# An adaLN block with linear attention and a GEGLU feed-forward: where the raw W_down transfers run, how many weight buffers gate/up has, and which queue loads the down weights

## The chip, the cores and the metric

The kernel runs on one core of one Trainium2 chip, as one program in one launch. The metric is the time of an execution in microseconds (us), read from the device. Several runs are made and their median counts.

A core has TensorE (PE, matmuls into PSUM), VectorE (DVE), ScalarE (ACT), GpSimd (POOL) and SyncE (SP, which here only issues DMAs). DMAs that POOL issues run through the "software" queue of the profile, those of SP and ACT through "hardware" queues; sixteen DMA engines serve all of them. Every engine works through its own instructions in order, so an instruction or a DMA issue that waits holds up all that stand behind it on that engine.

## The reference

S = 2048 rows, D = 1024, F = 3584, 32 heads of 32, all inputs bf16:

```python
mod = (_silu(c) @ w_mod).reshape(c.shape[0], 6, 1, -1)
sa, ca, ga, sb, cb, gb = (mod[:, 0].copy(), ..., mod[:, 5].copy())
h = _layernorm(x, axis=-1) * (1 + ca) + sa
x = x + ga * _A_ref(h, A_wqkv, A_wo)          # linear attention, phi = elu + 1
h = _layernorm(x, axis=-1) * (1 + cb) + sb
x = x + gb * _B_ref(h, B_w_gate, B_w_up, B_w_down)

def _B_ref(x, w_gate, w_up, w_down):
    return _gelu(x @ w_gate) * (x @ w_up) @ w_down
```

## The kernel before, in words

**Products.** Most matrix products are computed with seven block products in place of eight (the Strassen-Winograd form). That needs sums and differences of the blocks of both operands, which DVE makes, and sums of the products, which DVE and ACT make while they empty PSUM.

**Stages and their place in time.** The rows are cut into four blocks of 512. In the first stage (to about 160 us) each block's layer norm is followed by its K, V and Q products. `ln1_block(b)`, b = 1 to 3, loads four x tiles (SP, line 543), takes their statistics (DVE, 628 and 630), forms rstd and the bias (POOL, 635, 636 and 767), normalises (ACT, 769), stores the tile to `xa_scr[b]` (a DMA of POOL, 770) and, when all four are stored, loads the block back transposed (a DMA of SP, 771). DVE then scales and shifts it (775), and PE starts the block. Then come the merge of the attention state and the output projection (to about 247), and the feed-forward part for two groups of 1024 rows: `gate_up(0)` (247 to 422), `down_out(0)` (to 503), `gate_up(1)` (to 669), `down_out(1)`.

**Gate/up.** The weights come in 14 blocks of 1 MB, gate and up by turns (`w_unit`, load on SP, line 1295). A block needs four sums, s1 to s4, made on DVE by `tt_op` (550) during the block before. Three places in SBUF, `w_slots`, each hold one block and its four sums, so a block's load waits until PE is done with the block three before. In group 0, DVE also makes the sums of W_down (`wd_sums`): its loads (1066, 1067) stand in SP's queue between the weight loads, and POOL stores the results (1078, 1080). The next group's layer norm (`late_norm`) runs there too: a load on SP (1172), ACT, one POOL step (1179), a store by POOL (1182).

**Raw W_down transfers.** `wd_moves` issues from POOL, without passing SBUF, DMAs that write W_down's quarters into scratch in HBM: for each of two sums, 7 plain copies and 7 accumulating ones of 256 KB, 28 in all (line 1033). Ahead of each batch a one-element POOL copy (1053) reads a marker, so that the batch can't start before the marker's data are there. Fourteen run after block 3's transpose, two more with every second weight block of group 0.

**Down.** `down_out` loads W_down's blocks and their sums into regions that gate/up's buffers held (`quarters`, `W_AT`): `nested` products load seven small blocks on SP (1571), `plain` ones a single block of 1.75 MB (1533). In group 0, the three plain loads of sums ("t1", "t2", "t3") are issued by POOL; all others by SP. Residual tiles come by SP too (1521).

**Order.** The program is recorded as a list and `Plan` orders each engine's instructions: it simulates them forward and back with the costs in `cost`, and sorts by the starts it found. PE's order is that of the program. `plan.ahead` says how long before its due time a load may be placed.

Of the kernel before, what the change touches and what calls it, by code (L numbers as in the profile page):

```python
# [11 lines left out]
BF16 = mybir.dt.bfloat16  # L12
F16 = mybir.dt.float16
# [10 lines left out]
class Plan:  # L24
# [106 lines left out]
    def cost(self, op, outs, ins):  # L131

        size = lambda a: math.prod(d[1] for d in a.ap[1:])
        n = max(size(a) for a in (outs if op.eng == "PE" else outs + ins))
        psum = any(a.tensor.name.startswith("psum") for a in outs + ins)
        wide = any(a.dtype == FP32 and size(a) > 8 for a in outs + ins)
        ptrs = sum(size(a) == 1 for a in ins)
        if op.eng == "PE":
            op.cost = n / 2.4 + 2.5
            op.lat = op.cost + 165  # L140
            if op.fn == "matmul" and outs[0].ap[0][1] <= 32:
                op.cost /= 3.5
        elif op.fn.startswith("dma"):
            a = outs[0]
            op.cost, op.bytes = 1000 if op.eng == "POOL" else 450, math.prod(d[1] for d in a.ap) * (4 if a.dtype == FP32 else 2)
            op.bytes *= 2 if "accum_op" in op.kw else 1
            op.load = a.tensor.name.startswith("mem")
            if op.fn == "dma_start_transpose":
                op.cost, op.bytes = self.transpose
            op.lat = op.cost  # L150
        elif op.eng == "ACT":
            op.cost = (55 if psum else 112) + n / 1.2 + 85 * ptrs
            op.lat = op.cost + 115
            f = op.kw.get("func")
            op.table = "g" if f == AF.Gelu_apprx_tanh else "e" if f in (AF.Exp, AF.Ln) else None
        elif op.eng == "POOL":
            op.cost = 500 if n <= 8 else 250 + n / 0.46
            op.lat = 1800 if n <= 8 else op.cost
        else:
            rate = 1.0  # L160
            if op.fn in ("tensor_scalar", "tensor_scalar_mul", "tensor_scalar_add", "tensor_copy") and not wide:
                rate = 1.0 if psum else 4.0
            elif op.fn == "tensor_tensor" and not wide:
                rate = 2.0
            op.cost = 69 + n / (0.96 * rate) + 61 * ptrs
            op.lat = op.cost + 83

# [118 lines left out]
def kernel(  # L286
# [13 lines left out]
    nc = tc.nc  # L300
    P = 128
# [6 lines left out]
    KD = D // P  # L308
    JF = F // P
    TG = 512  # L310
    NG = S // TG
# [14 lines left out]
    KH = KD // 2  # L326
    NPR = JF // 2
    MW = 4 * NW

    KB = 1024  # L330
    mem_pool = ctx.enter_context(tc.tile_pool(name="mem", bufs=1))
    mem = mem_pool.tile([P, 103 * KB + KB // 2], BF16, name="mem", tag="mem")
    ps_pool = ctx.enter_context(tc.tile_pool(name="psum", bufs=1, space=bass.MemoryType.PSUM))
    psm = ps_pool.tile([P, 8, NW], FP32, name="psum", tag="psum")

# [48 lines left out]
    def at(off, shape, dt):  # L384
        return Ring(off, shape, dt, 1)()
# [61 lines left out]
    hr1 = [h12[b // 2][:, b % 2] for b in range(4)]  # L447
# [22 lines left out]
    nb_ring = Ring(206.75, [1], FP32, 8)  # L470
    sum_ring = Ring(206.25, [1], FP32, 8)

    w_slots = [(28, 44, 12), (28, 12, 44)]

    def quarters(n, shape, dt):

# [58 lines left out]
    plan = Plan(tc)  # L535
    te, ve, ac, gp, sy = (plan.on(e) for e in ("PE", "DVE", "ACT", "POOL", "SP"))
# [4 lines left out]
    def load_x(tt):  # L541
        xt = xt_ring()
        sy.dma_start(out=xt, in_=x_in[tt * P:(tt + 1) * P, :])
        return xt
# [80 lines left out]
    def ln_stats(xt):  # L625
        stats = bst_ring()
        for cb in range(NBN):
            ve.bn_stats(out=stats[:, cb, :], in_=xt[:, cb * BW:(cb + 1) * BW])  # L628
        mv = mv_ring()
        ve.bn_aggr(out=mv, in_=stats)  # L630
        return mv

    def pool_rstd(mv):
        rstd = rstd_ring()
        gp.tensor_scalar_add(out=rstd, in0=mv[:, 1:2], scalar1=1e-5)
        gp.tensor_tensor(out=rstd, in0=rstd, in1=nhalf, op=ALU.pow)
        return rstd
# [118 lines left out]
        return [lambda ch=ch: add(ch) for ch in range(2)]  # L756

    def ln1_block(b):
        plan.ahead = 4000 if b > 1 else 14000
        for tl in range(TT):  # L760
            xt = load_x(b * TT + tl)
            if b == 1:
                plan.chain.insert((1, 2, 5, 7)[tl], plan.ops[-1])
            mv = ln_stats(xt)
            rstd = pool_rstd(mv)
            nb = nb_ring()
            gp.tensor_scalar(out=nb, in0=mv[:, 0:1], scalar1=rstd, scalar2=-1.0, op0=ALU.mult, op1=ALU.mult)
            xh = xh_ring()
            ac.activation(out=xh, in_=xt, func=AF.Identity, scale=rstd, bias=nb)
            gp.dma_start(out=xa_scr[b][tl * P:(tl + 1) * P, :], in_=xh)  # L770
        sy.dma_start_transpose(out=hr1[b], in_=xa_scr[b][:])
        if b == NG - 1:
            wd_moves(hr1[b][:, 0, 0:1], NPR)
        for kd in range(KD):
            ve.tensor_scalar(out=hr1[b][:, kd, :], in0=hr1[b][:, kd, :], scalar1=opcA[:, kd:kd + 1],
                             scalar2=modT[:, kd:kd + 1], op0=ALU.mult, op1=ALU.add)
        plan.ahead = 14000
# [254 lines left out]
    def move(dst, src, add):  # L1032
        gp.dma_start(out=dst, in_=src, **(dict(accum_op=ALU.add) if add else {}))

    wd_q = {(fh, h): wd_v[fh][:, :, h * NW:(h + 1) * NW] for fh in range(2) for h in range(2)}
    wd_full = {"b11": wd_q[0, 0], "b12": wd_q[0, 1], "b21": wd_q[1, 0], "b22": wd_q[1, 1],
               **{f"t{j}": t_scr[:, j] for j in range(4)}}
# [9 lines left out]
    def wd_moves(seen_of, n):  # L1047


        if not wd_todo:  # L1050
            return
        plan.hold([op for op in plan.ops if op.eng == "PE"][-1])
        gp.tensor_copy(out=seen, in_=seen_of)
        plan.hold(plan.ops[-1])
        for dst, src, add in wd_todo[:n]:
            move(dst, src, add)
        del wd_todo[:n]
        plan.hold()
# [229 lines left out]

    def w_unit(g, n):

        wt = at(w_slots[g][n % 3], [2, KD * 4 * P], BF16)
        raw = wt[:, 0].rearrange("p (k e fh f) -> p k e fh f", k=KD, e=2, fh=2)
        sm = wt[:, 1].bitcast(F16).rearrange("p (s k e f) -> p s k e f", s=4, k=KH, e=2)
        j, wdr = n // 2, (B_w_gate, B_w_up)[n % 2]
        sy.dma_start(out=wt[:, 0].rearrange("p (k c) -> p k c", k=KD),
                     in_=wdr[:, j * 4 * P:(j + 1) * 4 * P].rearrange("(k p) c -> p k c", p=P))
        a11, a12 = raw[:, 0:KH, :, 0, :], raw[:, KH:KD, :, 0, :]
        a21, a22 = raw[:, 0:KH, :, 1, :], raw[:, KH:KD, :, 1, :]
        s1, s2, s3, s4 = (sm[:, j] for j in range(4))
        steps = [(s1, a21, a22, ALU.add), (s2, s1, a11, ALU.subtract), (s3, a11, a21, ALU.subtract),  # L1300
                 (s4, a12, s2, ALU.subtract)]
        w = dict(a11=a11, a12=a12, a22=a22, s1=s1, s2=s2, s3=s3, s4=s4, inner={})
        for name in INNER[g]:
            if n == 0 and name == "b11":
                continue
            x, at_w = (a11, wi_rings[0]()) if name == "b11" else (s1, wi_rings[1]())
            x11, x12, x21, x22 = (x[:, h * KH // 2:(h + 1) * KH // 2, e, :] for e in range(2) for h in range(2))
            q1, q2, q4 = (at_w[:, i] for i in range(3))
            q3 = x21.bitcast(F16) if name == "b11" else x21
            steps += [(q1, x21, x22, ALU.add), (q2, q1, x11, ALU.subtract), (q3, x11, x21, ALU.subtract),  # L1310
                      (q4, x12, q2, ALU.subtract)]
            w["inner"][name] = dict(x11=x11, x12=x12, x22=x22, s1=q1, s2=q2, s3=q3, s4=q4)
        w["steps"] = steps
        return w
# [194 lines left out]
    def down_out(g):  # L1509
        NC = 2  # L1510
        last = g == NGR - 1
# [18 lines left out]
        def plain(name, A, out, start):  # L1530

            wt = quarters(W_AT[g][name], [NPR, NW], F16 if name[0] == "t" else BF16)
            (sy if last or name[0] != "t" else gp).dma_start(out=wt, in_=wd_full[name])

            def mm(q, c):
                for i in range(NPR):
                    te.matmul(psm[:, q, c], lhsT=A[:, i, q * P:(q + 1) * P], rhs=wt[:, i, c],  # L1537
                              start=(start and i == 0), stop=(i == NPR - 1), skip_group_check=True)

            steps = []  # L1540
            for q in range(TT):
                parts = 2 if last and name == "t3" and q == TT - 1 else 1
                for n in range(parts):
                    c = slice(n * NW // parts, (n + 1) * NW // parts)
                    steps += [lambda q=q, c=c: mm(q, c), lambda q=q, c=c: out(q, psm[:, q, c], c)]
            return steps
# [222 lines left out]
```

## Time and profile before

| | us |
|---|---|
| median of 3 runs | 759.06 |
| lowest and highest run | 758.47, 765.38 |
| span of the profiled execution | 753.4 |
| first and last instruction to the run's time: median less this span | 5.7 |

| | before |
|---|---|
| DVE, ACT busy | 80%, 55% of the span |
| DMA, software queue (POOL) | 35.66 MB, 15.6% of 16 engines |
| DMA, hardware queue (SP) | 110.64 MB, 48.5% |
| SP's waits for PE ahead of gate and up loads | 212.1 us in 22 waits |
| raw W_down transfers | 28, issued from 107.2 to 383.2 us |

The profile is of one execution on the chip. Its views used here: the page; busy time of every engine in chosen stretches of the span (a stage's own picture); the timeline of one engine, with each group of instructions, its start and length, and in brackets how long the engine was idle before it and what ended that; the waits, who waited for whom; and the order of the built instructions on each engine. Matmuls overlap, so a matmul's own duration (379 ns for 512 columns) is longer than its share of time, about 216 ns.

### The profile page before, as it was taken

The page shows a single profiled execution, that of the slowest core. Times are in us where ns is not written, and L with a number is a line of the kernel's source. Part 1 is how long each engine was busy: PE and PEld are TensorE (multiplying, and loading weights), DVE is VectorE, ACT ScalarE, POOL GpSimd, SP SyncE. Part 2 cuts the span into 40 slices and gives each one's busy share as a digit, 9 for nine tenths or more (in the row PEclk, how much of TensorE's full clock was granted, in tenths as well). Part 3 has the DMA queues.
Part 4 walks back from the last instruction along what each step waited for, and adds up shares of the span by engine and source line. Part 5 has one row for each costly group of instructions (what it writes and reads, how often), then busy time and mean ns, then how long its engine had stood idle before and what let it go on. Part 6 is the DMA issues. An engine that isn't in the chain of part 4 may idle for free.

```text
span 753.4 us, 11454 instructions
## 1 busy us (share of the span) xinstructions
PE 731.7 (97%) x4150; PEld 388.7 (52%) x4164; DVE 602.9 (80%) x1304; ACT 417.6 (55%) x733; POOL 102.4 (14%) x179
## 2 busy tenths in 40 slices
PE   5999999999999999999999999999999999999997
PEld 2454545444444444444455486645555555548664
DVE  6898887587896899898975789678788888788763
ACT  2665586669213888976666362017776777741000
POOL 2321234000131143323110001110000000000000
PEclk9999999999999999999999999999999999999999
DMA  9837068817999779789544999561322313399822
GB/s 314 307 106 251 30 168 139 307 58 241 313 321 300 240 248 340 280 266 278 144 112 126 296 296 306 185 196 57 112 90 78 113 57 113 104 272 298 281 104 71
DMA packets 141689, 149.12 MB, mean 198 GB/s; under 512 B 33728, under 2 KB 121280, under 8 KB 140352
## 3 DMA queue, kind: packets, MB, share of 16 engines
q1 hardware_dynamic: 124944, 110.64, 48.5%
q0 software_dynamic: 14336, 35.66, 15.6%
q10 hardware_dynamic: 2352, 2.10, 0.8%
q8 instruction: 32, 0.52, 0.3%
q14 instruction: 25, 0.20, 0.1%
HBM read 116.00 MB, written 32.37 MB: 197 GB/s over the span
## 4 chain that ended last, share of the span: by engine, by line
PE 74%; DMA 9%; DVE 7%; ACT 6%; issue 2%; POOL 0%; SPq 0%; DVEq 0%; POOLq 0%; ACTq 0%
PE psum L1333 28%; PE psum L1537 13%; PE psum L1344 7%; PE psum L854 7%; PE psum L1581 6%; DVE mem L550 5%; PE psum L924 4%; PE psum L953 4%; DMA mem<-xhs 4%; DMA mem<-in_B_w_up_dram 2%; PE psum L677 2%; PE psum L1218 1%; DMA mem<-in_A_x_dram 1%; DMA mem<-in_B_w_gate_dram 1%; ACT mem L799 1%
## 5 line engine op out<-in xcount | busy, mean ns | idle before, releaser
L550 DVE TENSOR_TENSOR mem<-mem 128x512 f16<-128x512 f16 (+10 forms) x697 | 317.4, 502 | 34.4 <-ACT mem L799 13.0
L1333 PE MATMUL psum<-mem 128*128 128x512 f16 x1248 | 299.3, 379 | 0.7 <-ACT mem L799 0.2
L799 ACT ACTIVATE mem<-psum 128x512 f16<-128x512 f32 (+3 forms) x284 | 154.1, 563 | 109.2 <-PE psum L1581 44.4
L550 DVE TENSOR_TENSOR mem<-psum,mem 128x512 f16<-128x512 f32 (+4 forms) x204 | 154.9, 765 | 54.7 <-ACT mem L799 18.4
L1333 PEld LDWEIGHTS <-mem 128*128 128x128 f16 (+1 forms) x1248 | 122.0, 98 | 112.9 <-issue 3.1
L1537 PE MATMUL psum<-mem 128*128 128x512 f16 (+2 forms) x458 | 99.0, 372 | 0.7 <-DVE mem L550 0.5
L1344 PE MATMUL psum<-mem 128*128 128x256 f16 x560 | 89.5, 272 | 3.6 <-DVE psum L550 2.7
L1344 PEld LDWEIGHTS <-mem 128*128 128x128 f16 (+1 forms) x560 | 54.7, 98 | 49.7 <-issue 8.5
L1537 PEld LDWEIGHTS <-mem 128*128 128x128 f16 x462 | 45.2, 98 | 49.9 <-issue 0.7
L1581 PE MATMUL psum<-mem 128*128 128x256 f16 (+1 forms) x588 | 66.3, 273 | 1.0 <-ACT mem L799 1.0
L1581 PEld LDWEIGHTS <-mem 128*128 128x128 f16 x588 | 57.5, 98 | 10.4 <-issue 1.2
L854 PE MATMUL psum<-mem 128*128 128x512 f16 (+1 forms) x272 | 61.6, 379 | 0.4
L1387 ACT ACTIVATE psum<-psum 128x512 f32<-128x512 f32 x56 | 32.8, 586 | 48.0 <-PE psum L1333 28.9
L1218 PE MATMUL psum<-mem 128*128 128x512 f16 x256 | 56.3, 379 | 2.4 <-ACT mem L1015 1.5
L924 PE MATMUL psum<-mem 128*128 128x512 f16 x224 | 51.2, 379 | 0.4 <-ACT mem L894 0.2
L550 DVE TENSOR_TENSOR psum<-psum,mem 128x256 f32<-128x256 f32 x80 | 34.2, 428 | 18.0 <-ACT mem L799 17.3
L854 PEld LDWEIGHTS <-mem 128*128 128x128 f16 x280 | 27.1, 98 | 31.1
L1218 PEld LDWEIGHTS <-mem 128*128 128x128 bf16 x256 | 24.8, 98 | 33.1 <-issue 3.9
L1404 ACT ACTIVATE mem<-psum 128x512 f16<-128x512 f32 x56 | 33.0, 597 | 13.1 <-PE psum L1333 12.6
L1414 ACT ACTIVATE mem<-mem 128x512 f16<-128x512 f16 x56 | 34.6, 628 | 3.1 <-DVE mem L550 2.6
L924 PEld LDWEIGHTS <-mem 128*128 128x128 f16 (+1 forms) x224 | 21.5, 97 | 27.9 <-issue 3.3
L628 DVE BATCH_NORM_STATS2 mem<-mem 128x6 f32<-128x512 bf16 x48 | 31.0, 677 | 1.1 <-DMA mem<-in_A_x_dram 1.1
(127 smaller groups left out, 521.3 us busy)
## 6 DMA issues: line engine op xcount, KB each, us to landing
mem<-in_B_w_gate_dram SPq DMA_DIRECT2D x14, 1024.0 KB, 7.1
mem<-in_B_w_up_dram SPq DMA_DIRECT2D x14, 1024.0 KB, 6.5
mem<-in_w_mod_dram SPq DMA_DIRECT2D x24, 512.0 KB, 6.1
mem<-us SPq DMA_DIRECT2D x24, 448.0 KB, 7.2
mem<-in_A_x_dram SPq DMA_DIRECT2D x32, 256.0 KB, 5.3
ts<-in_B_w_down_dram POOLq DMA_DIRECT2D x28, 256.0 KB, 5.9
us<-mem POOLq DMA_DIRECT2D x7, 768.0 KB, 7.4
mem<-in_B_w_down_dram SPq DMA_DIRECT2D x12, 448.0 KB, 9.2
```

The source lines that it names most:

```text
L550: ve.tensor_tensor(out=out, in0=a, in1=b, op=op)
L799: ac.activation(out=t, in_=ps, func=AF.Copy)
L854: te.matmul(ps, lhsT=A[:, k, i * P:(i + 1) * P], rhs=B[:, k, :], start=(start and k == 0), stop=(k == KH - 1), skip_group_check=True)
L924: te.matmul(o, lhsT=W[:, k, (j0 + i) * P:(j0 + i + 1) * P], rhs=h_form(a, k), start=(start and k == 0), stop=(k == KH - 1), skip_group_che ...
L1218: te.matmul(psw[:, half, :], lhsT=pqT[b][:, g, tl * P:(tl + 1) * P], rhs=Wp[:, g, half * NW:(half + 1) * NW], start=(g == 0), stop=(g == K ...
L1333: te.matmul(ps, lhsT=a[:, k, e, :], rhs=b[:, k, :], start=(start and k == 0), stop=(k == KH - 1), skip_group_check=True)
L1344: te.matmul(ps, lhsT=self.x[a][:, k, :], rhs=self.y[y][:, k, :], start=(start and k == 0), stop=(k == KH // 2 - 1), skip_group_check=True)
L1387: ac.activation(out=z, in_=x, func=AF.Copy)
L1404: ac.activation(out=o, in_=ps, func=AF.Gelu_apprx_tanh)
L1414: ac.activation(out=o, in_=o, func=AF.Gelu_apprx_tanh)
L1537: te.matmul(psm[:, q, c], lhsT=A[:, i, q * P:(q + 1) * P], rhs=wt[:, i, c], start=(start and i == 0), stop=(i == NPR - 1), skip_group_chec ...
L1581: te.matmul(ps[:, q, :], lhsT=a[:, k, q * P:(q + 1) * P], rhs=y[:, k, :], start=(start and q == 0 and k == 0), stop=(k == NPR // 2 - 1), s ...
```

## The change

- The built program reserves 4 KB of each SBUF partition as scratch for descriptors of DMAs issued by POOL, where it had reserved the default. The kernel's own area grows by 12 KB, from 207 to 219 KB a partition.
- Group 0's gate/up has four places for weight blocks, group 1 keeps three. Each place is now a pair of offsets, the block's and that of three of its sums; the fourth sum, s3, overwrites its operand a21.
- The raw W_down transfers are issued in `ln1_block`: 7 after block 1's transpose, 11 after block 2's, 10 after block 3's. The marker is now the last column of the transposed block. None is left for `gate_up`, where `wd_moves` then returns at once.
- All down loads are issued by SP.
- In `Plan.cost`, `tensor_scalar_max` is taken as three times as fast; x loads of block 3 get a look-ahead of 14,000 ns where they had 4,000. Both alter the planned order alone.

In the built program PE's order and matmuls are the same. POOL's eight marker copies become three, and its three down loads go to SP. The x loads of block 3 stand ahead of the 2 MB weight load (547) on SP. Ahead of the down stage of group 0, the load for "b11" stands before those of the first nested product. After the second transposed load of that stage, SP's order is: "t1", six small blocks, "t2", the seventh, the residual tile of the second column half, "t3", the next residual, and then group 1's first weight blocks.

```diff
+            elif op.fn == "tensor_scalar_max":
+                rate = 3.0
...
-    mem = mem_pool.tile([P, 103 * KB + KB // 2], BF16, name="mem", tag="mem")
+    mem = mem_pool.tile([P, 109 * KB + KB // 2], BF16, name="mem", tag="mem")
...
-    w_slots = [(28, 44, 12), (28, 12, 44)]
+    w_slots = [((12, 20), (26, 34), (207, 54), (40, 48)), ((28, 36), (12, 20), (44, 52))]
...
     def ln1_block(b):
-        plan.ahead = 4000 if b > 1 else 14000
+        plan.ahead = 4000 if b == 2 else 14000
...
         sy.dma_start_transpose(out=hr1[b], in_=xa_scr[b][:])
-        if b == NG - 1:
-            wd_moves(hr1[b][:, 0, 0:1], NPR)
+        wd_moves(hr1[b][:, KD - 1, 0:1], (0, 7, 11, 10)[b])
...
     def w_unit(g, n):
-        wt = at(w_slots[g][n % 3], [2, KD * 4 * P], BF16)
-        raw = wt[:, 0].rearrange("p (k e fh f) -> p k e fh f", k=KD, e=2, fh=2)
-        sm = wt[:, 1].bitcast(F16).rearrange("p (s k e f) -> p s k e f", s=4, k=KH, e=2)
+        raw_at, sums_at = w_slots[g][n % len(w_slots[g])]
+        wt = at(raw_at, [KD, 4 * P], BF16)
+        raw = wt.rearrange("p k (e fh f) -> p k e fh f", e=2, fh=2)
...
-        s1, s2, s3, s4 = (sm[:, j] for j in range(4))
+        s1, s2, s4 = (at(sums_at + 2 * i, [KH, 2, P], F16) for i in range(3))
+        s3 = a21.bitcast(F16)
...
-            (sy if last or name[0] != "t" else gp).dma_start(out=wt, in_=wd_full[name])
+            sy.dma_start(out=wt, in_=wd_full[name])
...
-    nc = _bacc.Bacc("TRN2", target_bir_lowering=False, num_devices=1)
+    nc = _bacc.Bacc("TRN2", target_bir_lowering=False, num_devices=1, dynamic_dma_scratch_size=4096)
```

More of the change, by code (lines that the diff above doesn't have):

```diff
@@ L1289, in w_unit @@
     def w_unit(g, n):
-        wt = at(w_slots[g][n % 3], [2, KD * 4 * P], BF16)
-        raw = wt[:, 0].rearrange("p (k e fh f) -> p k e fh f", k=KD, e=2, fh=2)
-        sm = wt[:, 1].bitcast(F16).rearrange("p (s k e f) -> p s k e f", s=4, k=KH, e=2)
+        raw_at, sums_at = w_slots[g][n % len(w_slots[g])]
+        wt = at(raw_at, [KD, 4 * P], BF16)
+        raw = wt.rearrange("p k (e fh f) -> p k e fh f", e=2, fh=2)
         j, wdr = n // 2, (B_w_gate, B_w_up)[n % 2]
-        sy.dma_start(out=wt[:, 0].rearrange("p (k c) -> p k c", k=KD),
+        sy.dma_start(out=wt,
                      in_=wdr[:, j * 4 * P:(j + 1) * 4 * P].rearrange("(k p) c -> p k c", p=P))
```

## The prediction

> **What bounds the kernel now.** I read the page first, then busy time by stage, then the order of time around the stalls. Two lines of the page, span and busy totals:
>
> ```profile
> span 753.4 us, 11454 instructions
> ...
> PE 731.7 (97%) x4150; PEld 388.7 (52%) x4164; DVE 602.9 (80%) x1304; ACT 417.6 (55%) x733; POOL 102.4 (14%) x179
> ```
>
> TensorE (PE) is idle for 753.4 - 731.7 = 21.7 us in all, and the change alters no matmul. So the question is which of these 21.7 us it can reach. Busy time by stage (columns: stretch, length, then PE, PEld, DVE, ACT, POOL busy with instruction counts, granted clock, DMA share, GB/s) places them. First the twenty-microsecond stretches ahead of the feed-forward part:
>
> ```profile
> 40.00:60.00 20.00, 19.86 (x114) 10.04 (x116) 19.74 (x51) 14.45 (x22) 7.77 (x16) 1.00 0.31 97
> ...
> 80.00:100.00 20.00, 19.95 (x99) 9.32 (x99) 17.08 (x33) 13.55 (x16) 7.42 (x16) 1.00 0.13 48
> 100.00:120.00 20.00, 19.95 (x117) 9.94 (x116) 18.12 (x34) 15.52 (x18) 9.70 (x12) 1.00 0.87 162
> ```
>
> Then gate/up of group 0, about 12 us to a weight block:
>
> ```profile
> 296.00:308.00 12.00, 11.72 (x59) 5.63 (x58) 11.54 (x32) 8.82 (x18) 5.92 (x6) 1.00 0.96 321
> ...
> 321.00:333.00 12.00, 11.31 (x61) 5.71 (x59) 10.71 (x30) 8.34 (x17) 4.88 (x8) 1.00 0.89 227
> ...
> 346.00:360.00 14.00, 12.96 (x67) 6.41 (x66) 12.95 (x34) 6.55 (x14) 4.78 (x6) 1.00 0.77 210
> 360.00:372.00 12.00, 10.84 (x55) 5.17 (x53) 11.80 (x25) 9.49 (x18) 3.07 (x5) 1.00 0.74 176
> 372.00:384.00 12.00, 12.00 (x65) 6.10 (x63) 11.70 (x27) 6.73 (x14) 2.94 (x3) 1.00 0.37 95
> ...
> sum 175.00, PE 170.79 PEld 84.49 DVE 146.40 ACT 131.90 POOL 43.56; mean PE 12.20 PEld 6.04 DVE 10.46 ACT 9.42 POOL 3.11
> ```
>
> The reader is to see a loss of 175.00 - 170.79 = 4.21 us here, all before 372 us, where the DMA engines are busiest; after 372, PE loses nothing. The rest of the 21.7: 8.6 in the first 20 us, 3.4 from 20 to 247 (1.5 of it near 189, 0.9 near 236), 5.5 after 422 (4.1 in the last 13 us, 1.0 from 434 to 453). The granted clock is 1.00 throughout.
>
> VectorE's (DVE's) timeline names what is late in group 0; the bracket is its idle time and what ended it:
>
> ```profile
> 316.77 3.16 DVE L550 TENSOR_TENSOR mem<-mem 128x256 f16<-128x256 bf16 x8 [1.68 <-DMA mem<-in_B_w_up_dram]
> ...
> 341.88 3.77 DVE L550 TENSOR_TENSOR mem<-mem 128x256 f16<-128x256 bf16 x9 [1.35 <-DMA mem<-in_B_w_up_dram]
> ...
> 355.14 4.03 DVE L550 TENSOR_TENSOR mem<-mem 128x256 f16<-128x256 bf16 x9 [1.01 <-DMA mem<-in_B_w_gate_dram]
> ```
>
> After each late weight block DVE makes up eight or nine weight sums in a row, and PE waits behind them for the sums of a product (L550 into PSUM) at 322, 345 to 349 and 361. SyncE's (SP's) queue shows why the block was late:
>
> ```profile
> 304.48 0.42 SPq L1172 DMA_DIRECT2D mem<-x2s  x1
> 309.19 0.37 SPq L1295 DMA_DIRECT2D mem<-in_B_w_up_dram  x1
> ```
>
> SP is done at 304.9 and holds the load until 309.19, when the third weight buffer comes free of PE; nine such waits in this stage total 62.6 us.
>
> **Fourth buffer.** The waits on PE go; the next limit is the entry ahead of each load in SP's queue, whose order there is unchanged. That entry ends at 304.9, 328.4 and 339.2 for the three loads issued at 309.19, 334.01 and 346.81: earlier by 4.3, 5.6 and 7.6 us. DVE lacked them by 1.68, 1.35 and 1.01. The raw W_down loads (L1066, 40.5 us of waits on DVE) stay in front, so the loads do not run further ahead before 339. The third weight sum, now written over its own input, is the same DVE operation; no count changes. Of the 4.21 us, PE's waits on ACT (0.8) stay. I take 3.5 as gained; bounds 0 (if DVE, at 10.5 of 12 us, is itself the limit) and 4.2.
>
> **W_down transfers.** 28 transfers of 256 KB issue from POOL either way. Fourteen go out of group 0 (12 of them before 372, 12 x 0.25 = 3.1 of the 32.4 MB moved there), which also helps the loads; I add nothing for it. Five of eight marker copies (L1053, 0.2 to 0.7 us) go with them. What arrives ahead: 7 behind the transpose of block 1, 11 behind block 2's, 10 behind block 3's, all in POOL's queue before the rstd steps of the next block's layer norm. Price of one, from the fourteen that ran there before:
>
> ```profile
> 107.19 2.76 POOL L1033 DMA_DIRECT2D ts<-in_B_w_down_dram  x4
> ...
> 112.25 5.53 POOL L1033 DMA_DIRECT2D ts<-in_B_w_down_dram  x6 [0.33 <-issue]
> 122.61 3.47 POOL L1033 DMA_DIRECT2D ts<-in_B_w_down_dram  x3 [4.84 <-DMA ts<-in_B_w_down_dram]
> ```
>
> Fourteen in 107.19 to 126.08 is 1.35 us each with waits; single ones are 0.68 to 2.09. Block 2's transpose issues at 62.80 and DVE starts its scaling at 70.15. Block 1's lands by 35.59 + 7.3 = 42.9; six transfers end at 47 (0.69) to 51 (1.35), against 50.40 when the first rstd runs; the seventh stands between two rstd steps. So block 2 slips by 0.7 to 2.0 us. PE needs it at 74.26; its first four scalings are done at 71.53, a slack of 2.7. Cost nothing, covered by PE's block 1. Block 3: eleven from 70.4 hold POOL to 85.3 (bounds 77.9 and 93.4). From rstd (88.23) to the transpose (100.94) is 12.7, to DVE 7.35, four scalings 1.4, and PE needs them at 112.67: POOL must be free by 91.2. Cost nothing again, with 5.9 us to spare; at 2.09 each, 2.2 late. The x loads for block 3 move ahead of the 2 MB weight load (L547), whose sums DVE makes from about 92 us on, against 75.5 when it lands now, so its delay is hidden. Block 3's ten, from about 107 at 1.35 each, end near 121, before anything else asks POOL (160).
>
> [...]
>
> **Scratch of 4 KB.** The trace shows no transfer that waits for descriptor space. Bounds: 0, and a wait for every landing (5.9 us median), which holds POOL by 11 x 5.9 = 65 us to 135, 44 us late. A gain is excluded: it only frees memory. I take 0, by the nearest row, four transfers issued 0.69 apart with none landed. [...]
>
> **Down loads on SP.** Three loads leave POOL (issued at 440.57, 463.05, 475.20, each when its region came free) and now block SP until then. Behind the second stands the residual tile for the second output half (456.64 before, now after 463.1): the 1.75 MB ahead of it lands 7.4 us later, so about 472, and DVE first adds it at 472.7. Behind the third stand the next residual (needed about 485, lands about 484) and group 1's first weights (475.92 before, 475.6 now). In front, b11's load keeps 410.5, while five nested loads that went at 394 to 411 now wait for the last block's buffer, to 418 to 423; 5 x 448 KB at that stage's 268 GB/s land by about 432, and PE reads the first at 435.7. Cost 0, bounds -1.0 (the 434 to 453 stall) and +2.
>
> **Cost table, look-ahead.** No instruction; ACT and DVE swap neighbours in 40 to 245. I take 0, within -1.5 and +1.5 (the stall near 189).
>
> Sum: 753.4 - 3.5 = 749.9 of span; the median, 759.06, has 5.7 outside this span: **755.5 us**. One per cent, 7.6 us, is what I count as told from no change (three runs spread over 6.9).
>
> **Rivals.** (1) DVE is the limit in group 0 and not the weights: it is busy 12.95 of 14 and 11.80 of 12 us at the stalls; against it, it idled 1.0 to 1.7 just before each. Then 759. (2) The down stage pays: 758. (3) The slower one: POOL's queue holds block 3's layer norm past 91.2 us. With 2.09 us a transfer and the 2 MB weight load (8.8 us to landing) beside them, POOL is free at 102, PE stops 11 us, 766.5; at half of that excess 761. For it: POOL's late waits of 4.84 above; against it: DMA share 0.13 in 80 to 100. (4) The scratch stalls every transfer: about 800.
>
> **Numbers.** Forecast 0.55 (753 to 758), rival 1 0.17, rival 2 0.10, rival 3 0.15, rival 4 0.03. The range 752 to 764 leaves out the full price of rival 3, rival 4, and gains above 7. Faster by over 1% needs all bounds at once: 0.07. Slower by over 1%: rival 4, the top of rival 3, and slips not listed: 0.11. Within: 0.82.
>
> **What would show it.** DVE no longer waits on gate or up weights in 300 to 360, and PE's loss in 247 to 422 falls from 4.2 to under 1. Block 3's transpose issues before 105, and PE does not wait at block 2's or 3's start. The transfers keep 0.7 to 2.1 us. Wrong would be: a PE wait near 74 or 113, POOL issues far longer than 2 us, or DVE as late as before with weights already there.

## The result, and the profile after

| | before | after |
|---|---|---|
| median of 20 runs each, us | 760.93 | 767.92 |
| lowest and highest, us | 756.63, 768.10 | 758.54, 776.08 |
| span of the profiled execution, us | 753.4 | 774.3 |

The ratio after to before is 1.0064, with a 95% interval of 1.0034 to 1.0093: slower by some 5 us. It leaves out executions more than 1.5% above the fastest of their kernel, nine of the changed kernel's twenty and the profiled one among them, so the medians, 7.0 us apart, say more; both stalls shown below stand in executions that it counts too (transfers back, fourth buffer alone).

The page of the changed kernel (each digit is the busy share, or the granted clock, of one fortieth of the span):

```profile
span 774.3 us, 11442 instructions
...
PE 740.0 (96%) x4164; PEld 391.5 (51%) x4164; DVE 603.4 (78%) x1304; ACT 418.6 (54%) x733; POOL 102.7 (13%) x171
...
PE   5999999999993999999999979999999999999997
...
PEclk9999999999997899999999989999999999999999
```

TensorE (PE) is idle in two places, the 13th slice and the 24th, and its granted clock drops at both, to 7 and 8 tenths in the 13th and 14th slice and to 8 in the 24th. Busy time by stretch, before (columns as in the prediction):

```profile
220.00:240.00 20.00, 19.09 (x89) 8.59 (x88) 14.36 (x25) 6.74 (x12) 4.85 (x9) 1.00 1.09 273
240.00:260.00 20.00, 20.00 (x98) 9.40 (x97) 17.60 (x34) 14.30 (x25) 3.44 (x6) 1.00 0.77 263
260.00:420.00 160.00, 155.79 (x795) 77.34 (x793) 131.56 (x321) 120.36 (x229) 40.66 (x55) 1.00 0.75 230
440.00:460.00 20.00, 19.00 (x153) 14.69 (x151) 17.00 (x29) 12.68 (x20) 2.06 (x3) 1.00 1.11 295
```

and after:

```profile
220.00:240.00 20.00, 18.65 (x87) 8.36 (x86) 13.29 (x23) 1.00 (x4) 4.01 (x8) 1.00 1.14 196
240.00:260.00 20.00, 9.32 (x31) 3.60 (x31) 6.55 (x11) 7.26 (x10) 1.64 (x3) 0.66 1.06 246
260.00:420.00 160.00, 157.29 (x801) 78.15 (x800) 141.09 (x338) 122.80 (x231) 27.55 (x39) 1.00 0.58 197
440.00:460.00 20.00, 15.99 (x103) 10.18 (x102) 11.53 (x17) 5.88 (x11) 0.00 (x0) 0.95 1.13 279
```

Gate/up of group 0, where the change was to win, loses 160 - 157.29 = 2.71 us instead of 4.21. The end of the output projection (220 to 260) loses 12.0 instead of 0.9, at a clock of 0.66 in its second half; the start of the down stage 4.0 instead of 1.0.

**The first stall.** PE's, DVE's, ACT's and SP's timelines of the changed kernel, one fence each:

```profile
224.68 13.98 PE L1219 MATMUL psum<-mem 128*128 128x512 f16 x64
250.68 9.90 PE L1219 MATMUL psum<-mem 128*128 128x512 f16 x32 [12.02 <-DVE mem L552]
```

```profile
247.65 1.03 DVE L552 TENSOR_TENSOR mem<-mem 128x512 f16<-128x512 f16 x2 [14.36 <-ACT mem L1197]
...
249.41 2.35 DVE L552 TENSOR_TENSOR mem<-psum,mem 128x1024 bf16<-128x1024 f32 x2
```

```profile
246.10 5.75 ACT L1197 ACTIVATE mem<-mem 128x512 f16<-128x512 f16 x8 [20.54 <-DMA mem<-xhs]
```

```profile
217.53 0.43 SPq L1296 DMA_DIRECT2D mem<-in_B_w_gate_dram  x1
219.26 0.33 SPq L1214 DMA_DIRECT2D mem<-in_A_x_dram  x1
220.04 13.38 SPq L1155 DMA_TRANSPOSE mem<-xhs  x1
...
244.58 5.63 SPq L1155 DMA_TRANSPOSE mem<-xhs  x1
```

and SP's before:

```profile
213.83 0.43 SPq L1295 DMA_DIRECT2D mem<-in_B_w_gate_dram  x1
216.27 0.33 SPq L1213 DMA_DIRECT2D mem<-in_A_x_dram  x1
217.46 7.39 SPq L1154 DMA_TRANSPOSE mem<-xhs  x1
```

Read backwards: PE waits for DVE to empty PSUM (249.41). Ahead of that in DVE's order stand sums of the modulated rows (247.65), so DVE waits for ACT's modulation of the normalised rows (`h2_mod`, line 1197), and ACT waits for the transposed load of those rows (`h2_load(0, 0)`, line 1155). SP's order is the same in both kernels: the first gate block of 1 MB, an x tile, the transposed load. That load moves 4,096 packets of 256 bytes; counted among all DMA packets, its last one comes 25.2 us after its issue, against 13.4 before.

**The second stall**, SP's timeline of the changed kernel and of the kernel before, then ACT's and PE's of the changed one:

```profile
388.14 0.37 SPq L1296 DMA_DIRECT2D mem<-in_B_w_up_dram  x1
424.95 0.38 SPq L1535 DMA_DIRECT2D mem<-in_B_w_down_dram  x1
...
446.49 6.63 SPq L1155 DMA_TRANSPOSE mem<-xhs  x1
```

```profile
394.11 5.67 SPq L1571 DMA_DIRECT2D mem<-in_B_w_down_dram  x2
...
410.47 0.59 SPq L1533 DMA_DIRECT2D mem<-in_B_w_down_dram  x1
...
424.94 6.82 SPq L1154 DMA_TRANSPOSE mem<-xhs  x1
```

```profile
450.17 0.60 ACT L800 ACTIVATE mem<-psum 128x512 f32<-128x512 f32 x1 [0.93 <-PE psum L1583]
456.67 1.52 ACT L1197 ACTIVATE mem<-mem 128x512 f16<-128x512 f16 x2 [5.91 <-DMA mem<-xhs]
458.10 0.57 ACT L800 ACTIVATE mem<-psum 128x512 f32<-128x512 f32 x1
```

```profile
448.44 6.28 PE L1583 MATMUL psum<-mem 128*128 128x256 bf16 x56
458.72 15.27 PE L1583 MATMUL psum<-mem 128*128 128x256 f16 x112 [4.01 <-ACT mem L800]
```

After the last weight load SP stands still for 36.4 us, because the first entry of the down stage, the load of "b11" (424.95), waits for a place that the last gate/up blocks occupy; before, five small down loads stood ahead of that one and began at 394.11. The first stall has put this whole stage off, so times are best counted back from PE's first nested product (448.44 here, 433.98 before). The load of "b11" is 23.5 us ahead of it in both; but the small loads that came before it now come behind it, and the next group's transposed load behind them, 2.0 us ahead instead of 9.0. ACT has the modulation of those rows ahead of its second eviction of a product (L800), so it waits 5.91 us for the load, and PE waits 4.0 us for the eviction.

### The profile page after: what moved, and what is told of

Same layout as the page of the kernel before. It is cut to its first block, busy times and chain, and to the rows that moved or that the text cites. A ratio compares the mean times of both kernels' runs of the same rounds, so it can differ in the third digit from the quotient of the medians.

```text
span 774.3 us, 11442 instructions
## 1 busy us (share of the span) xinstructions
PE 740.0 (96%) x4164; PEld 391.5 (51%) x4164; DVE 603.4 (78%) x1304; ACT 418.6 (54%) x733; POOL 102.7 (13%) x171
## 5 line engine op out<-in xcount | busy, mean ns | idle before, releaser
L800 ACT ACTIVATE mem<-psum 128x256 f32<-128x256 f32 (+3 forms) x284 | 154.0, 562 | 110.8 <-PE psum L1583 44.3
L1583 PE MATMUL psum<-mem 128*128 128x256 f16 (+1 forms) x588 | 69.2, 279 | 4.0 <-ACT mem L800 4.0
L1219 PE MATMUL psum<-mem 128*128 128x512 f16 x256 | 59.2, 392 | 13.6 <-DVE mem L552 12.0
L1406 ACT ACTIVATE mem<-psum 128x512 f16<-128x512 f32 x56 | 33.2, 596 | 10.8 <-PE psum L1335 10.2
L1197 ACT ACTIVATE mem<-mem 128x512 f16<-128x512 f16 x28 | 20.8, 801 | 27.5 <-DMA mem<-xhs 27.5
L1416 ACT ACTIVATE mem<-mem 128x512 f16<-128x512 f16 x56 | 34.7, 627 | 1.1 <-DVE mem L552 0.5
```

The source lines that it names most:

```text
L800: ac.activation(out=t, in_=ps, func=AF.Copy)
L1219: te.matmul(psw[:, half, :], lhsT=pqT[b][:, g, tl * P:(tl + 1) * P], rhs=Wp[:, g, half * NW:(half + 1) * NW], start=(g == 0), stop=(g == K ...
L1406: ac.activation(out=o, in_=ps, func=AF.Gelu_apprx_tanh)
L1416: ac.activation(out=o, in_=o, func=AF.Gelu_apprx_tanh)
L1583: te.matmul(ps[:, q, :], lhsT=a[:, k, q * P:(q + 1) * P], rhs=y[:, k, :], start=(start and q == 0 and k == 0), stop=(k == NPR // 2 - 1), s ...
```

## The experiments

Every variant was timed in rounds with the kernel before on the same chip; "ratio" is to that, with its 95% interval. "Rows" is the time from the issue of the transposed load `h2_load(0, 0)` to its last packet, and "stalls" are the waits of PE for DVE in its output projection and for ACT in the nested down products (0 where the profile lists none), both from one profiled execution.

| variant | ratio | rows, us | stalls, us |
|---|---|---|---|
| changed kernel, again | 1.0074 (1.0030 to 1.0117) | 21.4 | 7.0, 4.1 |
| before + 4 KB scratch | 1.0003 (0.9962 to 1.0044) | 11.5 | 0, 0.8 |
| changed, transfers back | 1.0107 (1.0058 to 1.0157) | 19.7 | 8.6, 4.0 |
| changed, three buffers | 1.0010 (0.9976 to 1.0045) | 13.6 | 1.5, 2.6 |
| before + fourth buffer | 1.0091 (1.0046 to 1.0135) | 16.5 | 5.0, 7.4 |
| four buffers, order of three | 1.0070 (1.0028 to 1.0111) | 16.4 | 5.7, 4.2 |
| three buffers, order of four | 1.0116 (1.0053 to 1.0180) | 24.0 | 10.4, 2.1 |
| changed, gate load planned late | 0.9975 (0.9932 to 1.0018) | 10.2 | 1.0, 0.7 |
| changed, gate load moved | 1.0064 (1.0039 to 1.0088) | 6.8 | 1.6, 4.6 |
| before, gate load moved | 1.0005 (0.9980 to 1.0030) | 7.1 | 1.3, 0.5 |
| before, gate load nearer | 1.0056 (1.0013 to 1.0099) | 14.7 | 1.9, 1.5 |
| gate load moved, places rotated | 1.0014 (0.9987 to 1.0042) | 8.5 | 4.7, 0 |
| changed, places rotated | 0.9999 (0.9963 to 1.0035) | 16.1 | 4.0, 0 |
| planned late and rotated | 0.9962 (0.9932 to 0.9992) | 9.9 | 0.7, 0 |
| changed, down loads on GpSimd | 1.0219 (1.0178 to 1.0259) | 19.2 | 7.1, 7.7 |
| three buffers, planned late | 0.9977 (0.9954 to 1.0000) | 10.0 | 1.9, 0.7 |

### Which part of the change

The changed kernel, unaltered:

> The changed kernel once more, to see which of its stalls come back. If the stall of 12.2 us before the last part of the output projection (TensorE waits for the modulated rows, these for the transposed load of the normalised rows) belongs to the change, it is there again, 8 us or longer, and the time is 763 to 771 us beside 757 to 764 of the kernel before. If it is an accident of one execution, the stall is under 4 us here, and the time then shows what else the change costs: a median over 5 us above the kernel before would need another place in the profile.

Both stalls are there again. The first is 7.0 us here, short of the 8 expected, and 12.0 in the first execution: its length differs from one execution to the next, and the times spread (756.9 to 770.7 in 12 runs).

The kernel before with one line altered:

```diff
+    nc = _bacc.Bacc("TRN2", target_bir_lowering=False, num_devices=1, dynamic_dma_scratch_size=4096)
```

> The kernel before, with the scratch of 4 KB alone: every instruction stands where it stood. If the small scratch delays the stores and transfers that GpSimd issues (7.8 us to landing after, 5.9 us before), the transposed loads behind them are late here as well, and the ratio is 1.004 to 1.010. If the scratch costs nothing, as forecast, the ratio is 1.000 within 0.002 and the transfers land in 5.9 us again.

No cost that can be told from nothing: 1.0003 with an interval of 0.4% to both sides, and 5.9 us to landing as before.

The transfers back where they were:

```diff
-        wd_moves(hr1[b][:, KD - 1, 0:1], (0, 7, 11, 10)[b])
+        if b == NG - 1:
+            wd_moves(hr1[b][:, 0, 0:1], NPR)
```

> The changed kernel, with the W_down transfers put back where they were (14 behind the third block's layer norm, 14 in gate/up). If moving them costs the time, the ratio falls to 0.999 to 1.002. If the cause is the fourth buffer and its places, or the scratch, the ratio stays at 1.005 to 1.010; the transfers in gate/up would add nothing, as they added nothing before.

Both stalls stay, and the time: not the transfers.

Three places in group 0:

```diff
-    w_slots = [((12, 20), (26, 34), (207, 54), (40, 48)), ...
+    w_slots = [((12, 20), (26, 34), (40, 48)), ...
```

> The changed kernel without the fourth buffer in group 0: three places for the gate/up weights. If the fourth buffer lets weight loads go out early and these hold up the transposed loads of the output projection, the stall there is under 3 us and the ratio 0.998 to 1.003 (the 3.5 us that the buffer should win in gate/up are lost again, so 1.000 rather than 0.995). If the cause is the scratch or the transfers, the ratio stays at 1.005 or above, and gate/up loses about 4 us more: up to 1.012.

The loss is gone. But gate/up does not give back its gain: it loses 2.24 us between 260 and 420, with four buffers 2.71 and 2.25 in the two executions.

The reverse, the kernel before with the new places and the scratch (the diff is that of `w_unit`, `w_slots`, the kernel's area and the scratch in the change):

> The kernel before with the fourth buffer in group 0, its places and the scratch of 4 KB, and no other part of the change. If the buffer alone brings the late transposed load, TensorE waits 6 us or more at the end of the output projection and the ratio is 1.005 to 1.012. If it needs the moved transfers or the down loads on SyncE beside it, the stall is under 3 us and only the gain of gate/up is left, some 4 us: ratio 0.993 to 0.998.

The fourth buffer and its places alone bring both stalls, the first at 5.0 us and so short of the 6 expected. With it and the transfers in their old place gate/up loses 2.78 us, against 4.21 before.

### Order or place

The fourth buffer does two things: it occupies other places, and it makes the planner order the instructions ahead of gate/up anew. Up to the first matmul of gate/up, each engine was given the order of the other version, as a written list:

```diff
-        return [self.ops[n] for _, n in best[1]]
+        return [self.ops[n] for n in ORDER]
```

> The changed kernel with its four buffers, but up to the first matmul of gate/up every engine and queue runs in the order that the planner found for three buffers; from there on in the order of the changed kernel. If the planner's other order ahead of gate/up is what makes the transposed load late, the stall is under 3 us, gate/up keeps its gain of some 4 us, and the ratio is 0.994 to 1.000. If it is the places of the buffers, the stall is 6 us or more again and the ratio 1.004 to 1.010.

> The reverse: three buffers, but up to the first matmul of gate/up in the order that the planner found for four. If that order makes the transposed load late, the stall is 6 us or more and the ratio 1.007 to 1.014, above the changed kernel, since gate/up does not gain. If it is the buffers' places, the ratio stays at 0.999 to 1.004 as with three buffers in their own order.

Three buffers in the order of four are as slow as the changed kernel, with a first stall of 10.4 us: the buffer's places are not needed for it. Four buffers in the order of three should then have been free of it, and are not: 5.7 us in the profiled execution, with the second stall beside it. Up to there its program is that of the version with three buffers, which had 1.5. One execution of each can't tell a cause from a draw; how much the order adds was left there, and the load itself was moved.

### The gate load and the transposed load

The first gate block was held back until the transposed load had been placed, and the planner ordered the rest around it:

```diff
+        if (g, n) == (0, 0):
+            plan.hold(h2_loads[0, 0])
         sy.dma_start(out=wt,
                      in_=wdr[:, j * 4 * P:(j + 1) * 4 * P].rearrange("(k p) c -> p k c", p=P))
+        plan.hold()
```

> The changed kernel with the first gate weights of gate/up issued behind the first transposed load instead of 2.5 us ahead of it. If that 1 MB load in the queue ahead makes the transposed load late, the transposed rows land within 15 us of their issue (22 to 26 us in the changed kernel), the stall is under 3 us and the ratio 0.994 to 1.002, with up to 3 us lost at the start of gate/up where the weights come later. If the load is no cause, the stall is 6 us or more and the ratio 1.004 to 1.012.

Rows in 10.2 us, 1.0 us left of the first stall, 756.75 us beside 762.08. The second stall is nearly gone as well (0.7), which the load itself does not explain. Since the planner also altered other orders, the same was done by moving this one instruction, with every other in its place:

```diff
-        return [self.ops[n] for _, n in best[1]]
+        seq = [self.ops[n] for _, n in best[1]]
+        a, b = self.behind
+        seq.remove(a)
+        seq.insert(seq.index(b) + 1, a)
+        return seq
...
+        if (g, n) == (0, 0):
+            plan.behind = (plan.ops[-1], h2_loads[0, 0])
```

> The changed kernel, every instruction in its order but one: the first gate weights of gate/up (1 MB) are issued directly behind the first transposed load instead of 2.5 us ahead of it. If that load ahead is what lets the transposed load come late, the transposed rows land within 15 us of their issue, the first stall is under 3 us, and the ratio falls by 0.006 or more against the changed kernel, to 0.996 to 1.001; the second stall, of 4 us in the down stage, stays. If the version tried earlier won by the planner's other order and not by the load, the ratio stays at 1.004 or above.

> The kernel before with the same single instruction moved behind the first transposed load. If the long executions of the kernel before (a third of them, 763 us and more) are the same late transposed load, they become rare: the highest time stays under 763 us and the ratio is 0.992 to 0.998. If the load matters only in the changed kernel, ratio 0.999 to 1.003 with the same spread.

SP's and DVE's timelines of the changed kernel with the load moved (line numbers are four higher):

```profile
218.53 4.74 SPq L1159 DMA_TRANSPOSE mem<-xhs  x1
223.32 0.57 SPq L1300 DMA_DIRECT2D mem<-in_B_w_gate_dram  x1
```

```profile
232.34 0.69 DVE L556 TENSOR_TENSOR mem<-mem 128x1024 f16<-128x1024 bf16 x1 [3.38 <-DMA mem<-in_B_w_gate_dram]
```

The issue takes 4.74 us instead of 13.38 and the rows come in 6.8 us: the load ahead was what delayed them. What takes its place is seen in DVE's line: its first sum of gate weights now waits for the moved load. The time is another matter. The ratio, 1.0064, did not fall, which was the sign named for the planner's other order; the medians say a little more, 763.21 beside 758.80 (0.6%), against 767.44 beside 758.33 (1.2%, on another chip) for the changed kernel executed again. The second stall, 4.6 us, stays, so the 0.9975 of the planned version, which has 0.7 there, is not the load's alone. In the kernel before, the move gains nothing: 1.0005, and one run of 12 above 763 us against four of 30 unmoved is no difference that so few runs can show.

Then the other way, in the kernel before, one place nearer (`seq.index(b)` without the 1):

> The kernel before with that load issued directly ahead of the transposed load, one place later than it stands. If the changed kernel suffers more than the kernel before because its load stands closer to the transposed load (2.5 us ahead against 3.6 us), this version suffers too: rows land 18 us or more after their issue, stall 4 us or more, ratio 1.003 to 1.010. If closeness is not what counts, ratio 0.998 to 1.002.

The times fall into two groups, five runs at 758.0 to 759.0 and seven at 763.3 to 773.3 (unmoved, on the same chip, four of 30 were above 763). The profile was of the first group, with rows in 14.7 us and a stall of 1.9 where 18 and 4 were expected, so the long group itself was not seen; the time agrees with closeness, the profile does not decide.

### The places and the second stall

The moved load together with another rotation of the places, so that the last two blocks of gate/up no longer hold the places that "b11" and the first nested product need; and then the rotation alone:

```diff
-    w_slots = [((12, 20), (26, 34), (207, 54), (40, 48)), ...
+    w_slots = [((207, 54), (40, 48), (12, 20), (26, 34)), ...
```

> The changed kernel with the moved gate load, and with the four places handed out in another rotation, so that the places that the down stage loads first (7 to 21 KB) hold a unit before the last two of gate/up. If the second stall comes from SyncE waiting for these places (the down loads begin at 411 to 425 us, 394 us before) and so issuing the next transposed load late, the down loads begin by 405 us here, the second stall is under 1.5 us, and the ratio is 0.990 to 0.997, under that of the moved load alone by 0.003 or more. If the second stall has another cause, the ratio is that of the moved load alone within 0.002.

> The changed kernel with the four places handed out in the other rotation and nothing else. If SyncE's wait for the places of the last two units makes the second stall, the down loads begin by 405 us, the second stall is under 1.5 us, and the first stall stays; the ratio is then 1.000 to 1.005. If the places have no part in it, the second stall is 3 us or more and the ratio 1.006 to 1.011.

SP's and PE's timelines of the rotation alone:

```profile
395.35 8.19 SPq L1573 DMA_DIRECT2D mem<-in_B_w_down_dram  x2
...
435.94 6.34 SPq L1155 DMA_TRANSPOSE mem<-xhs  x1
```

```profile
442.97 18.57 PE L1583 MATMUL psum<-mem 128*128 128x256 bf16 x168
```

The down loads begin at 395, the transposed load is issued 7.0 us ahead of the first nested product (442.97 - 435.94; in the changed kernel executed again 1.6, before 9.0), and PE runs its 168 matmuls there without a wait. With the first stall still in it, the kernel is level with before. In the variant with the moved load the second stall is gone too, and its ratio is 0.005 under that of the moved load alone, but above the 0.997 expected: its first stall of 4.7 us is the wait for gate weights again.

Both mended, the load by the planner:

> The changed kernel with the first gate load behind the first transposed load, the planner told of it, and the places in the other rotation. If the two stalls are all that the change costs, what is left is the gain of gate/up: both stalls under 1.5 us, the transposed rows' last packet within 11 us of issue, ratio 0.991 to 0.997. If something else in the change costs time, the ratio stays above 0.998 though both stalls are gone.

Faster than the kernel before by 0.4%, the best of all and within the range expected. But the gain of gate/up is not what is left: 3.3 us of wait stand at its start, and PE loses 160 - 155.34 = 4.66 us from 260 to 420, more than before. The execution profiled is one of the longer ones (759.01 us), so the profile does not show where the 0.4% comes from. The second stall is gone in another way than by the rotation alone: the transposed load is issued 6.7 us behind the first nested product (446.19 and 439.49), but ACT now has five evictions of products (L800) ahead of the modulation. None of 12 runs was above 760 us, while the kernel before had six of 29 above 763 on that chip. DVE's timeline of this variant:

```profile
247.59 1.06 DVE L1199 TENSOR_SCALAR mem<-mem 128x512 f16<-128x512 f16 x3 [4.92 <-DMA mem<-xhs]
```

The gate load now stands ahead of the second transposed load, and that one's last packet comes 11.5 us after its issue, against 5.5 before; this pair was not tried apart.

### Two remaining parts

The three whole down loads back on GpSimd's queue:

```diff
-            sy.dma_start(out=wt, in_=wd_full[name])
+            (sy if last or name[0] != "t" else gp).dma_start(out=wt, in_=wd_full[name])
```

> The changed kernel with the three whole down loads back on GpSimd's queue as before. If moving them to SyncE has a share in the second stall, it falls under 2.5 us and the ratio drops by 0.003 against the changed kernel, to 1.002 to 1.006. If they cost nothing, as forecast, both stalls stay and the ratio is 1.005 to 1.011.

Neither: it is slower still, by 1.0% against the changed kernel executed again on the same chip, by the medians (775.38 and 767.44 us). GpSimd's (POOL's) timeline shows what comes late:

```profile
450.35 0.54 POOL L1535 DMA_DIRECT2D mem<-ts  x1 [77.39 <-PE psum L1583]
```

This load of 1.75 MB goes out 3.0 us ahead of the group's second transposed load (453.32), whose last packet then comes 12.6 us after its issue instead of 8.0. ACT waits 7.37 us for those rows and PE 4.6 us for ACT, a second wait in the same products behind one of 3.1. The kernel before with the fourth buffer, which also has these loads on GpSimd, shows the same pair (2.8 and 4.6). On SyncE the same load stands behind the transposed one.

Three buffers with the load planned late (the two diffs above together):

> The version with three buffers, and the first gate load behind the transposed load with the planner told of it. If the fourth buffer itself gains the 3 to 4 us in gate/up that it should, this version is slower than the one with four buffers and both stalls mended by 0.003 or more: ratio 0.996 to 1.001. If the gain comes from the new layout of the places and not from their number, it is level with it within 0.002.

Level with four buffers, 0.9977 against 0.9962, whose intervals overlap widely: what the fourth buffer itself is worth could not be told from nothing. In the profiles three buffers do better in gate/up: PE loses 1.93 us from 260 to 420, against 4.66 above and 4.25 with four buffers and the load planned late.

## Why the prediction was wrong, step by step

**The sum.** 755.5 us was forecast, 752 to 764 as the range; 767.92 came. Two steps failed. The down loads were put at nothing, and what stands behind them in SP's queue was not priced: PE waits 4.0 to 4.1 us there, before 1.0. And the wait at the end of the output projection had no term at all: 7.0 to 12.0 us, before 0.9. The fourth buffer's term was too large by 1.5 to 2.0 us; those of the transfers and the scratch held.

**Fourth buffer: 3.5 us gained.** Mis-sized. DVE's waits for weights in 300 to 360 were to go; two of three are left, in the changed kernel's timeline:

```profile
309.24 2.83 DVE L552 TENSOR_TENSOR mem<-mem 128x256 f16<-128x256 bf16 x7 [1.12 <-DMA mem<-in_B_w_up_dram]
...
333.31 4.37 DVE L552 TENSOR_TENSOR mem<-mem 128x256 f16<-128x256 bf16 x10 [0.85 <-DMA mem<-in_B_w_up_dram]
```

1.97 us against 4.04, and PE's loss of 4.21 falls to 2.71 and 2.25 in the two executions, by 1.5 to 2.0 us, not to under 1. SP's waits moved to the entry ahead, as the prediction had it, but there they grew: the raw W_down loads wait 64.7 us for DVE in all, before 40.5, and the late blocks stand behind them. Nor is the gain the buffer's alone. Three buffers with the transfers gone from this stage lose 2.24, four with the transfers in place 2.78 and 3.33, and the four-buffer versions with the load planned late 4.25 and 4.66. The prediction "added nothing" for 3.1 MB less to move. The kernel before itself loses 4.2 to 5.5 us in four executions of nearly the same program, so differences of 1 us say little. The real error is what the step left out: it followed the buffer to the loads behind it, not to whoever needs its place next.

**Down loads: cost 0, bounds -1.0 and +2.** Wrong. The prediction did see that b11's load would keep its time and that five nested loads would wait for the last block's buffer, and priced them by their own arrival in time for PE. It did not price what stands behind them in SP's queue, the transposed load of the next group, and behind that in ACT's queue, the eviction that PE needs: 4.1 us of wait, and most of the rest at a halved clock (the second execution loses some 7.5 us in 440 to 480, counted from matmul start to start at full pace, against some 1.3 before; its clock is 0.53 from 453 to 460). This is rival 2's place, the down stage, at more than its price of 758. The new queue itself, which the term was about, was no cost: with the loads on GpSimd the large one goes out ahead of a transposed load and the kernel takes 1.0% longer.

**The end of the output projection.** Not in the prediction at all; 0.9 us near 236 was listed among the losses and left there. It is the last sign of a wait with no margin: in the kernel before the rows came 13.4 us after their issue, PE had work for 18.4 (235.90, when it stopped, less 217.46), and modulation, sums and evictions used up what lay between. Of the three times known beforehand one stood out, 765.38 beside 758.47 and 759.06, and was taken for noise; no profile shows whether it was such a case.

**W_down transfers: cost 0.** Right, in part by luck. GpSimd's timeline after:

```profile
45.73 4.11 POOL L1034 DMA_DIRECT2D ts<-in_B_w_down_dram  x6
...
73.08 9.61 POOL L1034 DMA_DIRECT2D ts<-in_B_w_down_dram  x9
...
85.19 0.68 POOL L1034 DMA_DIRECT2D ts<-in_B_w_down_dram  x1 [0.75 <-DMA ts<-in_B_w_down_dram]
```

The eleven hold POOL to 85.87, forecast 85.3, but two errors cancel there: they start at 73.08 where 70.4 was taken, and take 1.16 us each where 1.35 was. Block 2's scaling starts at 72.81, 2.7 us later than before, the whole of the slack that was forecast. PE has no wait at block 2 or 3, and block 3's transposed load is issued at 98.15, before 105. Putting them back did not help (1.0107). One sign of being wrong did come, POOL issues far longer than 2 us, and meant nothing: single records last up to 4.02 us, but one starts about every 0.7 us while the others still run, and they end about 1.2 us apart. The eleven hold POOL for 12.8 us, and three transfers of block 1 that were issued wholly beside DVE's scaling (line 776, 46.78 to 49.60) took 0.68 us each, where rival 3 took 2.09. Rival 3 is refuted by that.

**Scratch: 0.** Right: 1.0003, and ten transfers are issued in 10.3 us without a wait.

**Cost table and look-ahead: 0 within 1.5.** Open. The new order ahead of gate/up is that of the planner with all edits together; with three buffers it is slow in the order of four, but the counterpart was not clean.

**What stays open.** That the gate load ahead of the transposed load delays the rows is shown: with it 11.5 to 25.2 us in twelve profiled executions, behind it 6.8 to 10.2 in six. Why the same order is late in most executions of the versions with four buffers, and only in some of the kernel before, is not: they differ by at most 1.2 us in how far ahead that load is issued, and not always in the same direction (4.6 us ahead where the transfers are back, 3.6 before). What the lateness alone costs in time is not shown either, since the versions that end it wait elsewhere instead, for gate weights or for the second transposed load. Sending that load some 70 us earlier, into a place that nothing else uses, where the queues run empty (DMA share 0.01 from 157 to 165 us of the changed kernel), was not measured.

## What to carry to other kernels

A transposed load that many instructions wait for should not be issued just behind a megabyte of something that is not urgent: look at what stands ahead of it in its own queue and in the others (here, rows in 11.5 to 25.2 us behind the megabyte and in 6.8 to 10.2 ahead of it). A new buffer is paid for by whoever loads into that place next; follow it through that queue to the last entry behind the wait, and through the in-order queue of the engine that waits for that entry (here SP stood still for 36.4 us, then ACT waited 5.91 and PE 4.0). And where a profile has a wait of a microsecond on a load that takes thirteen (0.9 and 13.4 us here), ask what happens in the execution in which it takes twenty (7.0 and 21.4).

## What the hardware showed

The late transposed load and the stores to HBM beside it were slow together. The packets of 256 bytes took 18 ns each in the second transposed load of the kernel before (4,096 in 4.2 us), 30 on average in its first one (rows in 13.4 us) and 48 in the first one of the changed kernel (25.2). The 4 KB packets of POOL's queue took 160 ns (before) and 162 (after) in the median of the whole execution, those of the stores beside the late load 279 on average from 232 to 245 us of the changed kernel. Stores alone were not enough for it: from 238 to 240 us of the kernel before, 58 such packets at 170 ns ran beside 1,690 of a transposed load at 18. In the changed kernel the packets of the gate load had ended by 226 us, and the rows came until 245; what keeps both slow is open.

A stall of PE cost more than its length. The clock by stretch in the changed kernel, around the first stall:

```profile
245.00:250.00 5.00, 0.00 (x0) 0.00 (x0) 1.96 (x4) 3.90 (x6) 0.00 (x0) 0.50 1.10 202
250.00:256.00 6.00, 5.33 (x13) 1.87 (x13) 1.75 (x2) 3.37 (x5) 1.09 (x2) 0.50 1.05 266
256.00:262.00 6.00, 6.00 (x28) 2.67 (x27) 4.05 (x8) 0.96 (x2) 0.54 (x1) 0.96 1.06 387
```

PE works again at 250.68, at half the clock until 256.4: 13 matmuls in 5.33 us, where 28 take 6.00 afterwards, some 2.5 us lost. Half the clock lasted 13.7 us around this stall of 12.0 (242.8 to 256.4) and 6.8 around the second, of 4.0 (457.8 to 464.7); by the clock of the stretches, about 6.8 at each stall of the second execution, of 7.0 and 4.1, and 3.4 with both mended, where the longest wait behind the first 20 us is 2.8. Over the whole span, the profiled executions with a wait of 2.8 us or more behind these 20 us have a mean clock of 0.987 to 0.998, those whose longest is 1.9 or less 0.999 or 1.000, and the one with the load planned late, whose longest is 2.6, 1.000.
